# Leftover tokens of two batches interleaved token by token and stored in one transfer

## The chip, the core and the metric

The kernel runs on one core of one Trainium2 chip. The metric is the device time of one execution in microseconds (us), as the median of several runs. The engines are TensorE (PE in the profile; its weight loads are PEld), VectorE (DVE), ScalarE (ACT), GpSimd (POOL) and SyncE (SP). SyncE, ScalarE and GpSimd can issue DMA transfers; a transfer that an engine issues stands in that engine's own queue of instructions, shown as SPq, ACTq or POOLq.

## What is computed

An attention with landmark keys (8 batches, 8 heads, 576 tokens, 64 wide, 32 landmarks), and behind it a gated feed-forward block on all 4608 tokens. Cut to what matters:

```python
a = softmax(phi)                                  # over the 32 landmarks
k_m = einsum('bhsm,bhsd->bhmd', a, k)
v_m = einsum('bhsm,bhsd->bhmd', a, v)
attn = softmax(q @ k_m.T / sqrt(64))
x = (attn @ v_m), heads side by side              # 4608 x 512
g = x @ w_gate                                    # 512 x 1536
h = g * sigmoid(g) * (x @ w_val)
out = h @ w_out                                   # 1536 x 512, float32
```

Row `576 b + t` of the output is token t of batch b.

## The kernel before

The kernel goes through the eight batches one after the other. For each it forms the attention weights, multiplies them with a product of values and feed-forward weights (tiles `t_U`), and makes the hidden layer h, transposed, in three chunks of 512 hidden units: `hts[b, c]`, a tile `t_h` of 128 partitions x 4 x 576 tokens in bf16. A token's place in `t_h` is its half: `r = 0, 1` picks one of two blocks of 288, and token `2 t + r` of the batch stands at place `t` of block r.

The last product, h times `w_out`, is done with seven products of blocks in place of eight (a scheme of Strassen's kind). It works on 256 of the 288 tokens of each half. So 512 tokens of each batch go through `products(b, ...)`, and the last 64 tokens of each batch are left over. The leftovers of four batches together make one more such set of products, a "quad": `products(b, (), 0)` for batches 0 to 3, run beside batch 4, and `products(b, (), 1)` for batches 4 to 7, which runs at the very end of the kernel.

The steps that touch the leftovers, in the order in which they run:

- `chunk_done(b, c)` is called when a chunk of a batch's hidden layer is ready. Its inner function `ends` (L592) copies the 64 leftover columns of that chunk, on GpSimd, into the tile `t_x`, of which there is one for each pair of batches: `xs[b // 2]`, 128 partitions x 12 x 128 columns. There are 24 such copies (8 batches, 3 chunks), each of 128 x 256 elements. Which of the 128 columns belongs to which token is what the change is about.
- `quad_sums(qd)` forms sums and differences of the two `t_x` tiles of a quad on GpSimd, twelve instructions of 128 x 256 elements (L664 for the first three, L560 for the other nine), into the tiles `t_Q` and, in part, back into `t_x`.
- `products(b, by_hand, quad)` multiplies slices of `t_x` and `t_Q`, as weights of 128 columns, with halves of `w_out` or of its differences `t_T` (L727). A column of `t_x` is a partition of the result, so one result block of 128 partitions holds the leftover tokens of two batches, 64 each.
- `leftover(name, room, half, cols)` takes each of the four result blocks of a quad (two pairs of batches, two halves of 256 output columns) out of PSUM with VectorE (L796, L339) and stores it. Two transfers of 64 rows x 1 KB go out for one block, by `store_leftover` (L687). Both are issued on SyncE, but for three of the four blocks at the very end: there the second half is issued on ScalarE's queue.

The instructions stand on each engine's queue in the order in which the Python code calls them. Transfers from SyncE and ScalarE take eight completion semaphores in turn, and a transfer waits until the one eight places earlier has landed. The other stores are those of `store_block` (L683, 256 or 512 KB, SyncE); SyncE also issues transposing transfers for queries and keys (L117, L284). Loads go by GpSimd's queue. At the end of the program (L1113) SyncE waits for all outstanding transfers, one semaphore after the other.

Of the kernel before, what the change touches and what calls it, by code (L numbers as in the profile page):

```python
# [10 lines left out]
BF16 = mybir.dt.bfloat16  # L11
# [3 lines left out]
def kernel(  # L15
# [19 lines left out]
    nc = tc.nc  # L35
# [3 lines left out]
    B, H, S, D = q.shape  # L39
# [6 lines left out]
    NJF = DF // 128  # L46
# [11 lines left out]
    hpool = ctx.enter_context(tc.tile_pool(name="hpool", bufs=2))  # L58
# [5 lines left out]
    out_b = out.rearrange("(b t) c -> b t c", b=B)  # L64
# [16 lines left out]
    def done(*tiles):  # L81

        for t in tiles:
            free.append(held.pop(id(t))[0])
# [250 lines left out]
    def copy(eng, out, in_):  # L335
        if eng == "a":
            nc.scalar.copy(out=out, in_=in_)  # L337
        else:
            nc.vector.tensor_copy(out=out, in_=in_)  # L339
# [217 lines left out]
    xs, Ss, late = {}, {}, []  # L557

    def subtract(eng, out, x, y):
        eng.tensor_tensor(out=out, in0=x, in1=y, op=ALU.subtract)  # L560
# [20 lines left out]
    def blocks(b, c):  # L581

        x = hts[b, c].rearrange("p (m e) t -> p e m t", e=2)
        return [x[:, e, :, HALF * n:HALF * n + 256] for n in range(2) for e in range(2)]

    def chunk_done(b, c):

        if b % 2 == 0 and c == 0:
            xs[b // 2] = hpool.tile([128, NJF, 2, 64], BF16, tag="xs", name="t_x")

        def ends():
            nc.gpsimd.tensor_copy(  # L592
                out=xs[b // 2][:, 4 * c:4 * c + 4, b % 2].rearrange("p o (t r) -> p o t r", r=2),
                in_=hts[b, c].rearrange("p o (r t) -> p o t r", r=2)[:, :, 256:],
            )

        t = upool.tile([128, 4, 2, 256], BF16, tag=f"U{c}" if b == 1 else f"S{c}", name="t_S")
        Ss[b, c] = t
        A11, A12, A21, A22 = blocks(b, c)

        def sums(eng, part=(0, 1, 2, 3)):
            if 0 in part:
                eng.tensor_tensor(out=t[:, 0], in0=A21, in1=A22, op=ALU.add)  # L603
            terms = ((t[:, 0], A11), (A11, A21), (A12, t[:, 1]))
            for n in part:
                if n:
                    subtract(eng, t[:, n], *terms[n - 1])

        end = c + 1 == NCH
        fourth = b in (3, 7)  # L610
        if (b, c) in ((0, 2), (1, 1), (1, 2)):
            late.append(lambda *part: sums(nc.gpsimd if b else nc.vector, *part))
        elif b < 2:
            sums(nc.gpsimd)
        elif end:
            sums(nc.vector)
            if b + 1 == B:
                second.pop()(nc.vector, (2, 3))
                wait_for(Ss[b, 1][0:1, 3, 0, 0:1])
            else:  # L620
                wait_for(t[0:1, 3, 0, 0:1])
                second.pop()(nc.gpsimd, (3, 2))
        else:
            if c:
                sums(nc.gpsimd, (0, 1))
                second.append(sums)
            else:
                sums(nc.gpsimd)
        if end and b > 1 and not fourth:
            late.append(ends)  # L630
        else:
            ends()
        if b > 1 and c == 1:
            loads(b + 3)
        if b + 1 == B and end:
            quad_sums(1)
        if (b, c) in beside_sums:
            beside_sums[b, c]()
# [3 lines left out]
    def wait_for(x):  # L642

        t = att.tile([1, 1], BF16, tag="mark", bufs=1, name="t_mark")
        nc.gpsimd.tensor_copy(out=t, in_=x)

    def quad_sums(qd):

        x, y = xs[2 * qd], xs[2 * qd + 1]

        def quarters(c):
            return (
                z[:, 4 * c:4 * c + 4].rearrange("p (m e) a t -> p e m (a t)", e=2)[:, e]
                for z in (x, y) for e in range(2)
            )

        for c in range(NCH):
            Qs[qd, c] = att.tile([128, 3, 2, 128], BF16, tag=f"Q{c}", bufs=1, name="t_Q")
        for n in range(4):
            for c in range(NCH):  # L660
                t = Qs[qd, c]
                A11, A12, A21, A22 = quarters(c)
                if n == 0:
                    nc.gpsimd.tensor_tensor(out=t[:, 0], in0=A21, in1=A22, op=ALU.add)  # L664
                elif n == 1:
                    subtract(nc.gpsimd, t[:, 1], t[:, 0], A11)
                elif n == 2:
                    subtract(nc.gpsimd, A21, A11, A21)
                else:
                    subtract(nc.gpsimd, t[:, 2], A12, t[:, 1])  # L670
# [11 lines left out]
        for u in parts:  # L682
            nc.sync.dma_start(out=rows[:, u], in_=t_o[:, u, cols])  # L683

    def store_leftover(t_o, b, cols, eng):

        eng.dma_start(out=out_b[b, 512:S, cols], in_=t_o)  # L687

    def products(b, by_hand, quad=None):

        h = DM // 2
# [3 lines left out]
        end = quad == 1 or (quad is None and b + 1 == B)  # L695

        def A(e, n):
            if quad is not None:
                return lambda c, m, u: xs[2 * quad + n][:, 4 * c + 2 * m + e].rearrange(
                    "p a t -> p (a t)"  # L700
                )
            return lambda c, m, u: hts[b, c][
                :, 2 * m + e, HALF * n + 128 * u:HALF * n + 128 * u + 128
            ]

        def Sx(n):
            if quad is not None:
                return A(0, 1) if n == 2 else lambda c, m, u: Qs[quad, c][:, min(n, 2), m]
            return lambda c, m, u: Ss[b, c][:, n, m, 128 * u:128 * u + 128]
# [73 lines left out]
            both("o2", 256, slice(0, DM))  # L783

        def leftover(name, room, half, cols):
            engs = (nc.sync, nc.scalar if end and name != "c11" else nc.sync)

            def run():
                if room:
                    t = mine[room, "all"][:, half]  # L790
                else:
                    t = work.tile([128, h], FP32, tag="to", name="t_o")
                home = mine[dict(c11="a", c12="c").get(name, "s")]
                other = dict(c11="p1", c22="p5", c12="q6").get(name)
                if other:
                    nc.vector.tensor_tensor(  # L796
                        out=t, in0=home[:, 0], in1=mine[other][:, 0], op=ALU.add
                    )
                else:
                    copy("v" if end else "a", t, home[:, 0])  # L800
                if name != "c22":
                    done(home)
                for k in range(2):
                    x = 4 * quad + 2 * (name > "c20") + k
                    store_leftover(t[64 * k:64 * k + 64], x, cols, engs[k])

            return run

# [2 lines left out]
            c11=c11, c22=c22, c12=c12, c21=c21,  # L811
        )
        if quad is not None:
            ops.update(
                c11=leftover("c11", None, 0, lo), c12=leftover("c12", "q6", 1, hi),
                c22=leftover("c22", "p5", 1, hi), c21=leftover("c21", "q6", 0, lo),
            )
        now = {n: f for n, f in ops.items() if n not in by_hand}
        first = product("s", A(0, 0), W_(0, lo), "p1") + product("a", A(1, 0), W_(1, lo), "c11")
        five = product("c", Sx(0), T(0), "p5")  # L820
        six = product("s", Sx(1), T(1), "q6")
        three = product("c", Sx(3), W_(1, hi), "c12")
        seven = product("s", Sx(2), T(2), "c22")
        four = product("s", A(1, 1), T(3), "c21")
        if quad is not None or b + 1 == B:
            return first + six + five + seven + three + four, ops
# [155 lines left out]
    def loads(b):  # L982

        if b < B:
            load_q(b)
            load_phi(b, nc.gpsimd)
            load_k(b)
            load_v(b)
# [7 lines left out]
    for b in range(2, B):  # L996
# [60 lines left out]
        quad = []  # L1057
        if b == 4:
            quad = products(b, (), 0)[0]
# [58 lines left out]
```

## Time and profile before

| | us |
|---|---|
| median of 3 runs | 233.81 (233.22 to 233.97) |
| span of the profiled execution | 231.4 |
| TensorE matmul busy | 221.6 (96%) |
| VectorE busy | 185.1 (80%) |
| ScalarE busy | 171.7 (74%) |
| GpSimd busy | 140.8 (61%) |

The span runs from the first to the last instruction that the profile shows, and the measured time contains some more around it. The table below is from the list of DMA issues: how often each kind of store occurs, its size, and the median time from issue to landing.

| store | queue | times | KB each | us to landing |
|---|---|---|---|---|
| `t_o` (L683) | SyncE | 11 | 512 | 3.0 |
| `t_o` (L683) | SyncE | 10 | 256 | 4.5 |
| `t_q` (L687) | SyncE | 6 | 64 | 2.0 |
| `t_o` (L687) | SyncE | 4 | 64 | 2.6 |
| `t_p` (L687) | SyncE | 3 | 64 | 1.9 |
| `t_q` (L687) | ScalarE | 2 | 64 | 2.2 |
| `t_p` (L687) | ScalarE | 1 | 64 | 2.2 |

In the lines of the profile, `out<-in` names the tiles written and read, `L592` is line 592 of the kernel, and the names in `out_dram<-t_q` are those of the tile that is stored. A line of the windows view gives, for a stretch of time, the busy time and the number of instructions of each engine, the clock that TensorE was granted (1.00 is all of it), the busy share of the 16 DMA engines, and GB/s. A line of the waits view names who waited, for what, and the total, number and longest of these waits.

### The profile page before, as it was taken

How to read it: one execution, taken by the hardware profiler on the slowest of the kernel's cores; microseconds unless marked ns; L12 is line 12 of the kernel's file. 1: busy time of each engine (PE TensorE's matmuls, PEld its weight loads, DVE VectorE, ACT ScalarE, POOL GpSimd, SP SyncE). 2: the span in 40 equal slices, each digit the busy share in tenths (PEclk: the TensorE clock that was granted, in tenths of full speed). 3: DMA queues.
4: the chain of work that ended last, by engine and by line, in shares of the span. 5: the costliest groups of instructions: out<-in, count | busy, mean ns of one | idle time of the engine just before them, and what ended most of it. 6: DMA issues, size and time to landing. Idle time of an engine off the chain costs nothing.

```text
span 231.4 us, 7210 instructions
## 1 busy us (share of the span) xinstructions
PE 221.6 (96%) x2825; PEld 169.8 (73%) x2825; DVE 185.1 (80%) x423; ACT 171.7 (74%) x365; POOL 140.8 (61%) x190
## 2 busy tenths in 40 slices
PE   6987799999999999999999999999999999999993
PEld 2544476778887777878788787887788778878882
DVE  4245789999966799989997668998999899977732
ACT  2777898988447989968896658978898789677310
POOL 8422427998199049765977689464845394039291
PEclk9999999999999999999999999999999999999998
DMA  6999999999996992999299946994014502202125
GB/s 214 210 211 206 199 207 207 221 245 268 205 225 175 256 256 49 223 204 184 71 223 191 226 134 115 252 236 89 28 65 114 104 0 95 91 10 84 31 85 160
DMA packets 36674, 36.84 MB, mean 159 GB/s; under 512 B 14624, under 2 KB 31008, under 8 KB 36640
## 3 DMA queue, kind: packets, MB, share of 16 engines
q0 software_dynamic: 16272, 22.42, 52.5%
q1 hardware_dynamic: 19600, 13.18, 22.9%
q10 hardware_dynamic: 768, 0.79, 1.1%
q8 instruction: 22, 0.36, 0.6%
q14 instruction: 12, 0.10, 0.1%
HBM read 42.47 MB, written 9.44 MB: 224 GB/s over the span
## 4 chain that ended last, share of the span: by engine, by line
PE 86%; DMA 9%; POOL 2%; ACT 1%; issue 0%; DVE 0%; POOLq 0%
PE p_g L515 21%; PE p_os L727 21%; PE p_v L515 20%; PE p_oc L727 10%; DMA W<-in_moe_w_val_dram 9%; PE p_oa L727 5%; PE p_u L472 5%; PE p_kv L230 2%; PE p_g L396 1%; POOL t_kv L99 1%; POOL t_kv L103 1%; PE p_q L383 0%; POOL t_q L108 0%; ACT t_qT L337 0%; POOL W L138 0%
## 5 line engine op out<-in xcount | busy, mean ns | idle before, releaser
L538 DVE TENSOR_TENSOR t_h<-t_sg,p_v 128x288 bf16<-128x288 bf16 x192 | 81.8, 451 | 14.1 <-PE p_v L515 7.0
L515 PEld LDWEIGHTS <-t_U 128*128 128x128 bf16 x768 | 73.9, 98 | 21.2 <-issue 3.5
L532 ACT ACTIVATE t_sg<-p_g 128x288 bf16<-128x288 f32 x192 | 73.3, 424 | 17.1 <-PE p_g L515 11.4
L515 PE MATMUL p_g<-t_A,t_U 128*128 128x288 bf16 x384 | 77.0, 286 | 0.0
L515 PE MATMUL p_v<-t_A,t_U 128*128 128x288 bf16 x384 | 77.0, 286 | 0.0
L727 PEld LDWEIGHTS <-t_S 128*128 128x128 bf16 x384 | 37.5, 98 | 4.5 <-issue 0.2
L603 POOL TENSOR_TENSOR t_S<-t_h 128x512 bf16<-128x512 bf16 x17 | 19.7, 1157 | 32.7 <-DVE t_h L538 31.2
L727 PEld LDWEIGHTS <-t_h 128*128 128x128 bf16 x288 | 27.1, 98 | 8.6 <-issue 5.0
L492 ACT CAST t_U<-p_u 128x512 bf16<-128x512 f32 x51 | 27.0, 605 | 6.6 <-PE p_u L472 6.6
L727 PE MATMUL p_os<-t_T,t_S 128*128 128x256 bf16 x192 | 23.7, 273 | 0.0
L560 POOL TENSOR_TENSOR t_S<-t_S,t_h 128x512 bf16<-128x512 bf16 x17 | 19.6, 1156 | 1.3
L560 POOL TENSOR_TENSOR t_S<-t_h 128x512 bf16<-128x512 bf16 x16 | 18.4, 1152 | 0.0
L560 POOL TENSOR_TENSOR t_S<-t_h,t_S 128x512 bf16<-128x512 bf16 x16 | 18.4, 1152 | 0.0
L472 PE MATMUL p_u<-W,t_kT 64*32 64x512 bf16 (+1 forms) x416 | 15.3, 363 | 1.2 <-DMA W<-in_moe_w_gate_dram 0.6
L496 DVE CAST t_U<-p_u 128x512 bf16<-128x512 f32 x21 | 13.6, 683 | 1.9 <-PE p_u L472 1.9
L727 PE MATMUL p_os<-t_T,t_h 128*128 128x256 bf16 x96 | 14.8, 273 | 0.0
L875 PE MATMUL p_warm<-bones 128*128 128x512 bf16 x44 | 12.5, 421 | 1.7 <-DVE bones L897 1.7
L452 DVE TENSOR_TENSOR t_A<-t_E,t_lz 128x576 bf16<-128x576 bf16 x16 | 11.4, 740 | 0.7 <-ACT t_lz L428 0.7
L727 PE MATMUL p_oc<-t_T,t_S 128*128 128x256 bf16 x96 | 11.9, 273 | 0.0
L727 PE MATMUL p_oa<-WO,t_h 128*128 128x256 bf16 x96 | 11.8, 273 | 0.0
L727 PE MATMUL p_oc<-WO,t_S 128*128 128x256 bf16 x96 | 11.8, 272 | 0.1
L727 PE MATMUL p_os<-WO,t_h 128*128 128x256 bf16 x96 | 11.8, 273 | 0.0
(107 smaller groups left out, 308.3 us busy)
## 6 DMA issues: line engine op xcount, KB each, us to landing
out_dram<-t_o SPq DMA_DIRECT2D x11, 512.0 KB, 3.0
t_kv<-in_k_dram POOLq DMA_DIRECT2D x8, 576.0 KB, 10.5
t_q<-in_q_dram POOLq DMA_DIRECT2D x8, 576.0 KB, 8.4
t_kv<-in_v_dram POOLq DMA_DIRECT2D x8, 576.0 KB, 14.7
t_phi<-in_phi_dram POOLq DMA_DIRECT2D x6, 576.0 KB, 8.1
out_dram<-t_o SPq DMA_DIRECT2D x10, 256.0 KB, 4.5
WO<-in_moe_w_out_dram POOLq DMA_DIRECT2D x3, 512.0 KB, 19.2
W<-in_moe_w_gate_dram POOLq DMA_DIRECT2D x2, 512.0 KB, 16.5
```

The source lines that it names most:

```text
L230: nc.tensor.matmul(p[g][32 * i:32 * i + 32, 0:n], lhsT=phi_of(b, g, j, i), rhs=kvs[b][64 * g:64 * g + 64, w0:w1, i, j * D:(j + 1) * D], st ...
L452: nc.vector.tensor_tensor(out=a, in0=es.pop((b, g)), in1=lzs.pop((b, g)), op=ALU.mult)
L472: nc.tensor.matmul(p[g][32 * i:32 * i + 32, o:o + n], lhsT=kTs[b][64 * g:64 * g + 64, 2, 32 * i:32 * i + 32], rhs=w_part(w, c, i, g, halve ...
L492: nc.scalar.copy(out=t, in_=p)
L496: nc.vector.tensor_copy(out=t, in_=p)
L515: nc.tensor.matmul(p[:, 0:HALF], lhsT=Us[b, c, g][:, o // 2, which, 128 * (o % 2):128 * (o % 2 + 1)], rhs=atts[b, g][:, r], start=(g == 0) ...
L532: nc.scalar.activation(out=sg, in_=gate[:, 0:HALF], func=AF.Silu)
L538: nc.vector.tensor_tensor(out=dst, in0=sg, in1=val[:, 0:HALF], op=ALU.mult)
L560: eng.tensor_tensor(out=out, in0=x, in1=y, op=ALU.subtract)
L603: eng.tensor_tensor(out=t[:, 0], in0=A21, in1=A22, op=ALU.add)
L727: nc.tensor.matmul(mine[home][:, u], lhsT=lhs(c, m, u), rhs=rhs(c, m), start=fresh and u == 0, stop=(k == 5), skip_group_check=u == 1 or n ...
L875: nc.tensor.matmul(p[:, 0:128 * a], lhsT=bones, rhs=x.to_broadcast([128, a, 128]) if a > 1 else bones, start=True, stop=True,)
```

## The change

The two batches of a pair change their places in `t_x`. Before, the first 64 columns were the tokens of the even batch and the next 64 those of the odd one. Now column `2 t + a` is leftover token t of batch a of the pair. The copy in `ends` writes every second column, from column 0 or 1, where it wrote 64 columns side by side; what it reads is the same. `quad_sums` and `products` see the same 128 columns in the new order. A result block so has the tokens of both batches on alternate partitions, and one transfer takes the whole block: its SBUF side is 128 partitions of 1 KB, its side in memory is 64 tokens x 2 batches x 1 KB. All eight are issued on SyncE; `store_leftover` and the use of ScalarE's queue fall away. In the built programs SyncE has 39 transfers where it had 44, ScalarE one where it had four; the order of all other work on each engine is the same.

```diff
     def chunk_done(b, c):
         if b % 2 == 0 and c == 0:
-            xs[b // 2] = hpool.tile([128, NJF, 2, 64], BF16, tag="xs", name="t_x")
+            xs[b // 2] = hpool.tile([128, NJF, 64, 2], BF16, tag="xs", name="t_x")
         def ends():
             nc.gpsimd.tensor_copy(
-                out=xs[b // 2][:, 4 * c:4 * c + 4, b % 2].rearrange("p o (t r) -> p o t r", r=2),
+                out=xs[b // 2][:, 4 * c:4 * c + 4, :, b % 2].rearrange("p o (t r) -> p o t r", r=2),
                 in_=hts[b, c].rearrange("p o (r t) -> p o t r", r=2)[:, :, 256:],
             )
...
         def quarters(c):
             return (
-                z[:, 4 * c:4 * c + 4].rearrange("p (m e) a t -> p e m (a t)", e=2)[:, e]
+                z[:, 4 * c:4 * c + 4].rearrange("p (m e) t a -> p e m (t a)", e=2)[:, e]
...
-    def store_leftover(t_o, b, cols, eng):
-
-        eng.dma_start(out=out_b[b, 512:S, cols], in_=t_o)
-
...
                 return lambda c, m, u: xs[2 * quad + n][:, 4 * c + 2 * m + e].rearrange(
-                    "p a t -> p (a t)"
+                    "p t a -> p (t a)"
                 )
...
         def leftover(name, room, half, cols):
-            engs = (nc.sync, nc.scalar if end and name != "c11" else nc.sync)
-
...
-                for k in range(2):
-                    x = 4 * quad + 2 * (name > "c20") + k
-                    store_leftover(t[64 * k:64 * k + 64], x, cols, engs[k])
+                x = 4 * quad + 2 * (name > "c20")
+                nc.sync.dma_start(
+                    out=out_b[x:x + 2, 512:S, cols].rearrange("a t c -> t a c"), in_=t
+                )
```

## The prediction

> **What bounds the kernel now.** I read the busy table first, then TensorE over its working stretch, then the chain that ended last, then the end of the span queue by queue, because the change touches stores and one small copy only.
>
> ```profile
> PE 221.6 (96%) x2825; PEld 169.8 (73%) x2825; DVE 185.1 (80%) x423; ACT 171.7 (74%) x365; POOL 140.8 (61%) x190
> ```
>
> ```profile
> core 0: us, PE busy (x) PEld busy (x) DVE busy (x) ACT busy (x) POOL busy (x), PEclk, DMA share, GB/s
> 27.00:227.60 200.60, 200.50 (x2517) 158.58 (x2493) 172.00 (x381) 153.77 (x336) 129.23 (x169) 1.00 0.74 154
> ```
>
> From 27.0 to 227.6 us TensorE is busy for 200.50 of 200.60 us at a granted clock of 1.00. No store and no GpSimd copy holds it up there. What the change saves in that stretch on any other queue is therefore worth nothing, unless it takes something away from TensorE. The order of TensorE's instructions is the same in both programs. The end, from 227.6 us on, is where a store can be seen:
>
> ```profile
> 226.88 0.73 PE p_os L727 x6
> 227.64 0.42 DVE t_q L339
> ```
>
> ```profile
> 223.68 0.38 SPq L683 DMA_DIRECT2D out_dram<-t_o  x1
> 226.76 0.47 SPq L687 DMA_DIRECT2D out_dram<-t_p  x1
> 226.76 0.55 ACTq L687 DMA_DIRECT2D out_dram<-t_p  x1
> 227.37 0.50 SPq L687 DMA_DIRECT2D out_dram<-t_q  x1
> 227.41 0.75 ACTq L687 DMA_DIRECT2D out_dram<-t_q  x1
> 228.14 0.47 SPq L687 DMA_DIRECT2D out_dram<-t_q  x1
> 228.28 0.54 ACTq L687 DMA_DIRECT2D out_dram<-t_q  x1
> ```
>
> The chain ends with the last product (227.6), VectorE's copy out of PSUM (ends 228.06) and two stores of 64 KB, one on SyncE's queue and one on ScalarE's. Columns are start, duration, engine, line. From issue to landing they take:
>
> ```profile
> out_dram<-t_o SPq DMA_DIRECT2D x1, 256.0 KB, 2.1
> out_dram<-t_q SPq DMA_DIRECT2D x1, 64.0 KB, 2.0
> out_dram<-t_q ACTq DMA_DIRECT2D x1, 64.0 KB, 2.2
> ```
>
> The landing events behind these rows are, to two places: SyncE 228.14 + 1.95 = 230.09, ScalarE 228.28 + 2.16 = 230.44. So ScalarE's half sets the end; it starts 0.14 later and takes 0.21 longer. SyncE waits for all stores one after the other:
>
> ```profile
> SPq L1113 <- DMA out_dram<-t_q: 1.0, 2, 0.7
> ```
>
> The span is 231.44 us, so 1.00 us follows the last landing. In the events ScalarE's semaphore is the last but one that SyncE asks for, and one more step of 0.06 us stands behind it. The median of the three runs, 233.81, lies 2.37 us above the span; I carry that over unchanged.
>
> **The change, part by part.** *Sixteen transfers become eight.* Eight leftover blocks went out as sixteen transfers of 64 KB: thirteen on SyncE, three on ScalarE. Now there are eight of 128 KB, all on SyncE. For the first quad, four pairs between 131.6 and 141.8 us become four singles: SyncE's queue gets some 4 x 0.59 = 2.4 us shorter. Behind them stand a 512 KB store and a transpose that feeds batch 5. They may start 0.6 us earlier, which TensorE's full stretch hides. The pair at 215.15 (1.12 us) has SyncE idle behind it until 218.81. Worth 0.
>
> *The end.* ScalarE loses three issues, 0.55 + 0.75 + 0.54 = 1.84 us; nothing is queued behind them but the end of the program. The last store is now one SyncE issue at 228.14, as before (it waits for VectorE, not for the queue, while one issue takes less than 0.7 us). Its form, 128 partitions on one side and 64 steps of 2 rows on the other, is in no row, so I bound issue to landing from both sides. How fast the halves move is seen here:
>
> ```profile
> 224.50:225.50 1.00, 1.00 (x11) 0.88 (x10) 0.47 (x1) 0.37 (x1) 1.00 (x2) 1.00 0.77 262
> 227.80:228.70 0.90, 0.00 (x0) 0.00 (x0) 0.26 (x1) 0.00 (x0) 0.00 (x0) 1.00 0.76 180
> ```
>
> The last two numbers are the share of the DMA engines and GB/s. The 256 KB store from 128 partitions (first line) moves 262/0.77 = 340 GB/s when busy, which over 16 engines is 48 ns for a row of 1 KB. The stores from 64 partitions (second) move 180/0.76 = 237 GB/s, 69 ns a row. One block has 128 rows, 8 for each engine; a half has 4; the 256 KB store has 16. Low bound: the 256 KB row less eight rows, 2.13 - 8 x 0.048 = 1.75. High bound: SyncE's half plus its whole stretch of movement again (0.45 us in the packet records), 1.95 + 0.45 = 2.40. The nearest row is the 256 KB one (same partitions, same 1 KB rows). But the outer count of 64 belongs to the slower issues: 0.47 against 0.38, and the first row moved 1.12 against 0.89 us after the start. I add that 0.23 to the low bound: 1.98. So landing at 228.14 + 1.98 = 230.12, against 230.44: -0.32. The 0.06 step behind ScalarE's semaphore falls away, since the last semaphore is now the last asked for: -0.38 in all. With the bounds, -0.61 to +0.04.
>
> The Trainium skill, DMA: Bandwidth & Descriptors, has two places that bear on this. "Rules for kernel authors" says not to split a transfer into partition halves, on two queues either, because both share the same engines; the rows of 69 and 48 ns go with it, and it speaks for the change. Its fit in "Anatomy of one DMA", about 2.0 us plus bytes over 436 GB/s (for GpSimd's path), speaks against: 131072 bytes make an estimate of 2.30 us, a landing at 230.44, and a gain of nothing but the 0.06. The measured 256 KB store took 2.13 where the fit says 2.60, so I go by the trace.
>
> *The copy on GpSimd.* All 24 copies of leftover columns now write every second element:
>
> ```profile
> L592 POOL COPY t_x<-t_h 128x256 bf16<-128x256 bf16 x24 | 10.3, 435 | 0.0
> L664 POOL TENSOR_TENSOR t_Q<-t_x 128x256 bf16<-128x256 bf16 x6 | 3.8, 658 | 0.0
> ```
>
> The number of elements stays 256, and the source was read with a stride already, so I take 0 more. No row shows a strided write; bounds are 0 and the 0.22 to the two-input row of the same size (a packed write gone could even double 0.41; that is a rival). The cover: until 210 us GpSimd's work is hidden under TensorE. In the last batch only the copy at 218.36 counts, since GpSimd waits 4.2 us for VectorE before it. Twelve sums follow back to back, and the last is close to its reader:
>
> ```profile
> 224.38 1.92 POOL L560 TENSOR_TENSOR t_Q<-t_x,t_Q 128x256 bf16<-128x256 bf16 x3
> 226.06 0.82 PE L727 MATMUL p_oc<-WO,t_Q 128*128 128x256 bf16 x6
> ```
>
> It ends at 226.30. The fifth of these six products begins at 226.50 and its weights load 0.1 earlier, so 0.1 us is spare. A copy 0.22 longer would push the end by 0.12.
>
> *Sum.* -0.38 + 0 + 0: span 231.06, time 231.06 + 2.37 = 233.43. With the bounds, -0.61 + 0 and +0.04 + 0.12: 233.2 to 234.0.
>
> **The rivals.** *The new form is slow to issue (slower).* The place is SyncE's queue after 226.76. Three leftover stores follow each other there, and if an issue takes X, the third starts at 226.8 + 2X + waits. What speaks for it: both sides of every SyncE copy so far have the same counts, here they differ (128 against 64 x 2), and the 64-count issue is already the dearer one. Against: no plain issue on SyncE after 80 us exceeds 0.6 us but one of 1.03, behind traffic. If an issue costs as much as the pair it replaces, 1.12 to 1.19, the three start at 226.76, 227.99 and 229.22; the last ends at 230.41 and lands some 1.5 to 1.8 later (1.95 - 0.47, and up to 0.28 for four more rows), near 232.05. That is +1.6 us, 235.4. It decides (over 0.70 us) from X of about 0.9 on. The same price would come from a transfer spread over few engines.
>
> *GpSimd's strided write costs double.* 0.41 more on the copy at 218.36, less the 0.1 spare, holds the last products up by 0.31 and eats the gain: 233.43 + 0.31 = 233.7. For it: it is an untried form on an engine with 0.1 us of slack. Against: it moves one element per partition at a time anyway by its 0.41 us for 256, as far as a duration can tell.
>
> *The transfer is as long as ScalarE's half.* Twice as many rows in one queue at 69 ns land at 2.30 to 2.40: the end stays, 233.8.
>
> *More gain than I see.* Over 0.70 us faster would need a landing at 229.7, 1.6 us after the issue, faster than any store in the trace. Only scatter (the three runs span 0.75 us) or another chip's run can give that.
>
> **How the numbers follow.** Forecast 0.47, copy dear 0.12, no gain 0.10, slow issue 0.22, more gain 0.09. A change under 0.3% (0.70 us) can't be told from none in such measurements. Forecast, copy and no gain lie all within it, but for scatter: same 0.62. Faster 0.14 is the last case and 0.05 of scatter from the forecast. Slower 0.24 is the slow issue and 0.02 of scatter. The predicted time is 233.5, the forecast's 233.43 rounded. The range reaches from 232.9 (forecast's low end and 0.3 of scatter) to 235.3, nearly the whole of the slow issue.
>
> **What would show it.** Right: eight SyncE stores of 128 KB, each issued in 0.4 to 0.6 us and landing within 1.75 to 2.4; none on ScalarE; 27 to 227.6 us still full; the copies at 0.41; the last landing 230.0 to 230.4. Wrong: issues over 0.9 us, a gap before the last eighteen products, or any new wait of TensorE in the middle.

## The result, and the profile after

| | median us | runs | range of the runs |
|---|---|---|---|
| before | 233.41 | 21 | 233.07 to 234.00 |
| changed | 232.94 | 21 | 232.75 to 233.66 |

The ratio is 0.9985 with an interval of [0.9978, 0.9991]: the change gains 0.15%, about 0.35 us (0.2 to 0.5 by the interval; the medians differ by 0.47). That is a gain, but within the 0.3% named in the prediction as no change. The profiled execution of the changed kernel has a span of 231.18 us, where the kernel before had 231.44.

The page's busy table of the changed kernel is nearly the old one:

```profile
PE 222.2 (96%) x2825; PEld 170.0 (74%) x2825; DVE 184.8 (80%) x423; ACT 171.4 (74%) x365; POOL 141.4 (61%) x190
```

Two windows of the changed kernel follow, TensorE's working stretch and half a microsecond in which only the last store moves:

```profile
27.00:227.60 200.60, 200.50 (x2517) 158.59 (x2501) 171.72 (x381) 153.62 (x336) 129.86 (x169) 1.00 0.72 154
229.40:229.90 0.50, 0.00 (x0) 0.00 (x0) 0.00 (x0) 0.00 (x0) 0.00 (x0) 1.00 0.78 260
```

TensorE is as full as before, 200.50 of 200.60 us, so nothing was gained or lost in the middle. In the second line 260 GB/s at a share of 0.78 is 333 GB/s when busy. Over 16 engines that makes 49 ns for a row of 1 KB. The new store moves at the rate of the 256 KB stores, not at the 69 ns of the old halves.

The end of the changed kernel in the timeline (start, duration, engine, line; then idle time ahead and its releaser):

```profile
224.48 1.91 POOL L560 TENSOR_TENSOR t_Q<-t_x,t_Q 128x256 bf16<-128x256 bf16 x3
...
226.14 0.81 PE L723 MATMUL p_oc<-WO,t_Q 128*128 128x256 bf16 x6
...
226.84 0.55 SPq L798 DMA_DIRECT2D out_dram<-t_p  x1
...
227.48 1.27 SPq L798 DMA_DIRECT2D out_dram<-t_q  x2
227.72 0.42 DVE L339 COPY t_q<-p_os 128x256 f32<-128x256 f32 x1 [0.30 <-PE p_os L723]
```

GpSimd's last sum ends at 226.39, inside the six products that read it, and holds none of them up. One transfer goes out for each block, on SyncE alone; the line "x2" holds the issues at 227.48 and 228.20, of 0.56 and 0.54 us. The list of DMA issues (KB each, median us to landing) and the wait at the end, both of the changed kernel:

```profile
out_dram<-t_q SPq DMA_DIRECT2D x4, 128.0 KB, 2.1
out_dram<-t_p SPq DMA_DIRECT2D x2, 128.0 KB, 2.1
```

```profile
SPq L1108 <- DMA out_dram<-t_q: 0.5, 1, 0.5
```

A store of 128 KB lands about as soon after its issue as the 256 KB one did before (2.1). SyncE now waits for one landing where it waited for two.

To compare kernels at a few tenths of a microsecond I use three events of each trace: the end of VectorE's last copy out of PSUM, the landing of the last store (its last semaphore event), and the end of the span. What comes before the copy is TensorE's chain, whose end differs by 0.12 us between the two profiles of the changed kernel (the copy ends at 228.14 and, in c1 below, at 228.26); what follows it is the tail that the change works on. Microseconds:

| kernel | copy ends | copy to last landing | landing to end | copy to end |
|---|---|---|---|---|
| before | 228.06 | 2.38 | 1.00 | 3.38 |
| changed | 228.14 | 2.12 | 0.92 | 3.04 |

The tail is 0.34 shorter: 0.26 by the store, 0.08 behind its landing. That is as much as the measured gain of 0.35.

The packet records of the two profiles divide the 0.26. Counted from the end of the copy, ScalarE's half was issued after 0.22 us and the new store after 0.06. The first row moves 1.27 and 1.19 us after the issue, the rows take 0.45 and 0.52, and the landing follows the last row by 0.44 and 0.35. So the rows of the new store take 0.07 longer than those of the half. What is gained is that the half on ScalarE, which was issued later and took longer to its first row and from its last row to the landing, is no longer needed, and what makes that possible is that 128 rows take little longer than 64; at the pace of the halves they would take about 0.9 (an estimate, 2 x 0.45).

### The profile page after: what moved, and what is told of

It reads as the page before. It is cut to its first block, busy times and chain, and to the rows that moved or that the text cites. A ratio compares the mean times of both kernels' runs of the same rounds, so it can differ in the third digit from the quotient of the medians.

```text
span 231.2 us, 7197 instructions
## 1 busy us (share of the span) xinstructions
PE 222.2 (96%) x2825; PEld 170.0 (74%) x2825; DVE 184.8 (80%) x423; ACT 171.4 (74%) x365; POOL 141.4 (61%) x190
## 4 chain that ended last, share of the span: by engine, by line
PE 86%; DMA 9%; POOL 2%; ACT 1%; issue 0%; DVE 0%; POOLq 0%
PE p_g L515 21%; PE p_os L723 21%; PE p_v L515 20%; PE p_oc L723 10%; DMA W<-in_moe_w_val_dram 9%; PE p_oa L723 5%; PE p_u L472 5%; PE p_kv L230 2%; PE p_g L396 1%; POOL t_kv L99 1%; POOL t_kv L103 1%; PE p_q L383 0%; POOL t_q L108 0%; ACT t_qT L337 0%; POOL W L138 0%
## 5 line engine op out<-in xcount | busy, mean ns | idle before, releaser
L870 PE MATMUL p_warm<-bones 128*128 128x512 bf16 x44 | 13.3, 444 | 1.7 <-DVE bones L892 1.7
L723 PE MATMUL p_os<-t_T,t_h 128*128 128x256 bf16 x96 | 14.8, 273 | 0.0
```

The source lines that it names most:

```text
L723: nc.tensor.matmul(mine[home][:, u], lhsT=lhs(c, m, u), rhs=rhs(c, m), start=fresh and u == 0, stop=(k == 5), skip_group_check=u == 1 or n ...
L870: nc.tensor.matmul(p[:, 0:128 * a], lhsT=bones, rhs=x.to_broadcast([128, a, 128]) if a > 1 else bones, start=True, stop=True,)
```

## The experiments

All twelve in one table, with the same three intervals and with the time against the kernel before, measured beside it. (For b4 the copy is VectorE's half of it.)

| run | copy to landing | landing to end | copy to end | median us | ratio to before |
|---|---|---|---|---|---|
| a1_end_only | 2.16 | 1.16 | 3.33 | 233.34 | 0.9993 [0.9982, 1.0004] |
| a2_first_only | 2.27 | 1.70 | 3.97 | 233.99 | 1.0025 [1.0014, 1.0035] |
| a3_halves | 2.44 | 0.97 | 3.42 | 233.52 | 0.9997 [0.9986, 1.0007] |
| a4_two_steps | 9.13 | 0.94 | 10.07 | 248.81 | 1.0665 [1.0640, 1.0690] |
| c1_changed_again | 2.13 | 0.92 | 3.05 | 232.91 | 0.9981 [0.9972, 0.9989] |
| x1_one_more | 2.12 | 1.84 | 3.95 | 233.94 | 1.0021 [1.0010, 1.0032] |
| x2_first_only_four_more | 2.34 | 0.97 | 3.31 | 233.55 | 0.9999 [0.9986, 1.0012] |
| x3_end_only_four_more | 2.52 | 0.93 | 3.45 | 233.49 | 1.0008 [0.9993, 1.0024] |
| x4_end_only_four_fewer | 2.12 | 0.94 | 3.06 | 233.18 | 0.9993 [0.9972, 1.0014] |
| b1_sync_halves | 4.19 | 0.92 | 5.10 | 235.42 | 1.0086 [1.0065, 1.0107] |
| b2_copy_twice | 2.13 | 0.94 | 3.07 | 233.45 | 0.9997 [0.9982, 1.0013] |
| b4_copy_shared | 2.44 | 0.92 | 3.37 | 233.29 | 0.9991 [0.9977, 1.0005] |

**The last quad alone, the first quad alone.** If the gain is the last store's, changing only batches 4 to 7 keeps it and changing only batches 0 to 3 loses it.

```diff
-            xs[b // 2] = hpool.tile([128, NJF, 64, 2], BF16, tag="xs", name="t_x")
+            xs[b // 2] = hpool.tile([128, NJF, 128], BF16, tag="xs", name="t_x")
...
+    TOGETHER = (1,)        # a1_end_only;  (0,) in a2_first_only
+    def by_batch(b):
+        form = "p j (t a) -> p j a t" if b // 4 in TOGETHER else "p j (a t) -> p j a t"
+        return xs[b // 2].rearrange(form, a=2)
...
+                if quad in TOGETHER:
                     nc.sync.dma_start(
                         out=out_b[x:x + 2, 512:S, cols].rearrange("a t c -> t a c"), in_=t
                     )
+                    return
+                engs = (nc.sync, nc.scalar if end and name != "c11" else nc.sync)
+                for k in range(2):
+                    engs[k].dma_start(out=out_b[x + k, 512:S, cols], in_=t[64 * k:64 * k + 64])
```

> New order of columns and single stores for batches 4 to 7 alone; batches 0 to 3 as before. Theory (the gain is made after the last product, by the last store): all of it, 0.3 to 0.4 us under the kernel before (ratio 0.9985), last landing about 2.1 us after the end of VectorE's last copy against 2.38 before. Rival (the gain comes from SyncE's shorter queue between 131 and 142 us): 0.0, ratio 1.000.

> New order and single stores for batches 0 to 3 alone; the end of the kernel as before, with three halves on ScalarE's queue. Theory: no gain, ratio 1.000 within 0.001; SyncE's queue 2 us shorter between 131 and 142 us, TensorE full there as before. Rival (SyncE's queue in the middle): 0.9985.

The store did what was expected in both. In a1 it lands 2.16 after the copy (2.12 in the changed kernel), in a2 the old pair takes 2.27 (2.38 before). The whole did not follow: the tail of a1 is 3.33, hardly shorter than the 3.38 of before (its time, 0.9993, lies in an interval that holds the whole gain and none), and a2 is slower than before. The table says where it went: behind the landing, 1.16 and 1.70 us in place of 0.92. So I listed what SyncE does there. It asks for the semaphores of the last transfers one after the other, in a fixed order (the walk, below). These are the times at which the trace has each request, which is when its semaphore has come (the number is the semaphore's):

```
before  106 228.65  108 229.13  109 229.22  113 229.29  114 229.35  115 229.64  116 229.70  117 230.46  118 230.52
changed 106 228.79  108 228.85  109 228.91  113 228.98  114 229.07  115 229.14  116 229.64  117 229.73  118 230.28
a1      106 228.91  108 228.98  109 229.47  113 229.69  114 230.42  115 230.48  116 230.55  117 230.61  118 230.67
a2      106 229.59  108 230.58  109 230.65  113 231.29  114 231.36  115 231.85  116 231.93  117 232.00  118 232.06
```

Two things are in this list. Each request costs 0.06 to 0.09 us, so it matters on which semaphore the last landing falls. In the changed kernel it is 118, the last asked for (landing 230.26, request 230.28). In a1 it is 114 (230.40), with four requests behind it; in a2 it is 113 (231.28), with five. And in each list one step of 0.49 to 0.50 us has no landing to wait for: 106 to 108 before, 115 to 116 in the changed kernel, 108 to 109 in a1, 114 to 115 in a2. Counted along SyncE's recorded instructions it always follows the 79th. Before and after the change it lies while SyncE would wait for the last landing anyway; in a2 it lies behind the landing and is paid. Both places depend on the number of transfers in the whole program. The semaphores are given out in turn, in rounds of eight. The kernel before has 48 transfers on SyncE and ScalarE, six rounds; the changed kernel has 40, five rounds, so its last store is on 118 again. a1 and a2 have 44, and end half way through a round. Neither kernel changed only what it was meant to.

**The walk tested.** Four kernels change that number by splitting or joining 512 KB stores in the middle, where TensorE is full. x1 is the changed kernel with one transfer more, 41 in all, so that the last store falls on 108, the first of the eight asked for. x2 and x3 are a2 and a1 with four more (48), x4 is a1 with four fewer (40).

```diff
-        parts = [slice(u, u + 1) for u in range(2)] if b < 2 else [slice(0, 2)]
+        apart = b < 2 or (b, n) in ((6, 1),)                              # x1
+        apart = b < 2 or (b, n) in ((4, 1), (5, 1), (6, 0), (6, 1))       # x2, x3
+        parts = [slice(u, u + 1) for u in range(2)] if apart else [slice(0, 2)]
...
+        parts = [slice(0, 2)]                                             # x4
```

> The changed kernel, but the 512 KB store of batch 6 near 207 us goes out as two of 256 KB. Nothing stands behind it on SyncE for 8 us. It makes one transfer more, so the last store falls on the first of the eight completion semaphores that SyncE asks for at the end, not on the last. Theory (where the last store stands in that order counts, 0.06 us for each semaphore asked for after it, and a pause of about 0.45 us in SyncE's queue there may come out from under the landing): 0.43 to 0.9 us slower than the changed kernel, ratio to before 1.0004 to 1.0024. Rival (only the transfer counts): as the changed kernel, 0.9985.

> The changed kernel once more, beside the three that follow. Ratio 0.9985 within 0.0008 by every theory.

Measured in the same set of runs: 233.94 against 232.91, so one transfer more costs 1.03 us (0.93 by the two ratios), nearly three times what the change gains. The wait view of x1, to be held against the 0.5 of the changed kernel:

```profile
SPq L1109 <- DMA out_dram<-t_q: 1.4, 1, 1.4
```

SyncE waits longer because it now waits at the first of the eight. In the events the landing is at 230.10, then the requests for 108 to 118 stand at 230.12, .19, .25, .32, .81, .89, .96 and 231.02: seven steps, and the pause of 0.46 again between 114 and 115, behind the 79th instruction. Together they take 0.91 us.

> New form for batches 0 to 3 alone, as in the run that came out at 1.0025, but four 512 KB stores after 160 us go out as two of 256 KB each, so that the last stores fall on the same semaphores as in the kernel before. Theory (that run lost its 0.58 us in the walk through the semaphores at the end): 1.000 within 0.001. Rival (the new form itself holds TensorE up near 135 us): still 1.002 to 1.003.

x2's tail is 3.31 and its ratio is back at 0.9999. The loss of a2 was the walk and the pause, not the old stores and not the new form in batches 0 to 3.

> New form for batches 4 to 7 alone, with the same four stores split, so that the last store falls on the last semaphore asked for, as in the changed kernel, where it was the fourth of eight. Theory: the whole gain, 0.9985 within 0.001, against 0.9993 without the four. Rival (half of the gain comes from batches 0 to 3): 0.9993 again.

This one missed: 1.0008 where 0.9985 was expected. The walk is short (0.93 behind the landing), as planned, but the landing itself is late, 2.52 behind the copy. The timeline of x3:

```profile
228.11 1.64 SPq L805 DMA_DIRECT2D out_dram<-t_q  x2
228.32 0.42 DVE L339 COPY t_q<-p_os 128x256 f32<-128x256 f32 x1 [0.30 <-PE p_os L729]
```

The pair of issues that takes 1.27 us in the changed kernel takes 1.64 here. The first is over at 228.65, the copy ends at 228.75, and the last store is issued at 229.20 only. With four transfers more, the 79th instruction is the last store but one, and the pause stands right ahead of the last store. I had moved the semaphore and overlooked that the pause moves too.

> New form for batches 4 to 7 alone, and the stores of batches 0 and 1 whole (512 KB) where they went out as two, so four transfers fewer than in the end-only run: the last store again falls on the last semaphore asked for, and the pause of about 0.45 us in SyncE's queue, which has stood ahead of its 82nd instruction in all traces so far, falls between the last two of these semaphores, under the landing. (With four transfers more, the 82nd instruction was the last store itself.) Theory (the whole gain is made by the last store, if the pause stays hidden): 0.9983 within 0.001, 3.05 us from the end of VectorE's last copy to the end of the span. Rival (batches 0 to 3 bring part of the gain): 0.9993 or more.

By time x4 decides nothing: its interval holds 0.9985 and 1 alike. Its profile has the tail that was expected, 3.06, with the last store on 118 and nothing paid behind it. (The place that the expectation counts as the 82nd is the 80th of the instructions that the trace records, the one behind the 79th as above.) So changing the last quad alone gives the whole shorter tail if the count comes out well; that its time does too is not shown.

**Interleaved, but still in two halves.** a3 keeps the new layout and splits each block into two transfers of 64 partitions (32 tokens x 2 batches), the second on ScalarE's queue as before.

```diff
-                nc.sync.dma_start(
-                    out=out_b[x:x + 2, 512:S, cols].rearrange("a t c -> t a c"), in_=t
-                )
+                engs = (nc.sync, nc.scalar if end and name != "c11" else nc.sync)
+                for k in range(2):
+                    rows = slice(512 + 32 * k, 544 + 32 * k)
+                    engs[k].dma_start(
+                        out=out_b[x:x + 2, rows, cols].rearrange("a t c -> t a c"),
+                        in_=t[64 * k:64 * k + 64])
```

> New order of columns everywhere, but each block still goes out in two transfers of 64 partitions, 32 tokens of both batches each, the second halves at the end on ScalarE's queue. Theory: no gain, ratio 1.000 within 0.001 (last landing 2.3 to 2.4 us after VectorE's last copy), and 69 ns for a row of 1 KB; the interleaving itself is worth nothing. Rival (the new order of columns or of rows in memory is what is faster): 0.9985 or part of it.

The time is that of before, 0.9997 [0.9986, 1.0007], and the tail 3.42. The window of its last stores:

```profile
228.10:229.00 0.90, 0.00 (x0) 0.00 (x0) 0.17 (x1) 0.00 (x0) 0.00 (x0) 1.00 0.77 184
```

184 GB/s at a share of 0.77 is 239 GB/s when busy, 69 ns a row: the rate of the old halves. That two halves move side by side is not the reason: in b1 below, where they follow each other on SyncE alone, the rows of one half still take 0.45 to 0.47 us in the packet records, against 0.51 to 0.53 for the twice as many rows of the new store. A window of b1 in which only its last half moves:

```profile
231.80:232.20 0.40, 0.00 (x0) 0.00 (x0) 0.00 (x0) 0.00 (x0) 0.00 (x0) 1.00 0.67 154
```

That is 230 GB/s when busy, 71 ns a row. So the order of the tokens in itself gives nothing; it is the single transfer over all 128 partitions that moves its rows faster and makes ScalarE's half unnecessary.

**One transfer, but not interleaved.** a4 keeps the layout of before and stores a block as 2 batches x 64 tokens in one transfer.

```diff
-                for k in range(2):
-                    x = 4 * quad + 2 * (name > "c20") + k
-                    store_leftover(t[64 * k:64 * k + 64], x, cols, engs[k])
+                x = 4 * quad + 2 * (name > "c20")
+                nc.sync.dma_start(out=out_b[x:x + 2, 512:S, cols], in_=t)
```

> Order of columns as before, each block in one SyncE transfer whose side in memory is 2 batches x 64 tokens. Theory (what makes the single transfer good is its spread over all DMA engines; the outer count of 64 allows that, an outer count of 2 allows two engines): the last store takes 64 rows of 48 to 70 ns on each engine, 3.1 to 4.5 us, and lands 4.5 to 6 us after its issue; the three last stores queue up behind each other, 3 to 10 us slower than before. Rival (any single transfer of 128 partitions moves at 48 ns a row over all engines): as fast as the changed kernel, ratio 0.9985.

It is 15.2 us slower, more than the 3 to 10 that I expected. A window of a4's end:

```profile
239.00:245.00 6.00, 0.00 (x0) 0.00 (x0) 0.00 (x0) 0.00 (x0) 0.00 (x0) 0.62 0.14 48
```

A store of the same 128 KB, which moved at 260 GB/s in the changed kernel, moves at 48, at a share of 0.14, close to 2 of 16 engines (0.125). The last three stores land 4.98, 7.10 and 9.06 us after their issues, one behind the other. That makes the tail 6.7 us longer. The rest is in the middle, where the timeline of TensorE in a4 has

```profile
150.75 0.71 PE L727 MATMUL p_oc<-WO,t_S 128*128 128x256 bf16 x5
157.05 1.22 PE L727 MATMUL p_os<-t_T,t_S 128*128 128x256 bf16 x5 [5.59 <-ACT t_q L752]
```

TensorE waits 5.59 us for ScalarE, whose copy waits until a slow store of the first quad has left the `t_q` buffer. The windows of a4 behind this wait show the granted clock:

```profile
150.00:157.00 7.00, 1.46 (x14) 1.17 (x12) 2.39 (x5) 1.12 (x2) 3.59 (x7) 0.86 0.99 175
...
158.00:159.00 1.00, 1.00 (x7) 0.67 (x6) 0.00 (x0) 0.30 (x1) 0.00 (x0) 0.50 0.45 139
...
162.00:164.00 2.00, 2.00 (x21) 1.42 (x20) 1.69 (x4) 1.52 (x5) 0.00 (x0) 1.00 0.79 127
```

For some five microseconds TensorE runs at half its clock. The tail (6.7), the wait (5.6) and about 2.5 for the clock (an estimate, half of five) make 14.8 of the 15.2. I had counted the slow transfer at the end and not the buffer that it holds in the middle. The Trainium skill, DMA: Bandwidth & Descriptors, section "Why a DMA increments its semaphore by 16 and not by 1", says that a transfer spreads over the largest number of engines, up to 16, that divides the slowest dimension of both its sides. That gives 2 for a4's memory side of 2 x 64 and 16 for the interleaved one of 64 x 2; the share of 0.14 agrees.

**Without ScalarE's queue, without the interleaving.** b1 is the kernel before with both halves on SyncE.

```diff
-            engs = (nc.sync, nc.scalar if end and name != "c11" else nc.sync)
+            engs = (nc.sync, nc.sync)
```

> The kernel before, with both halves of each block on SyncE at the end too. Theory: SyncE issues six halves of 0.47 to 0.58 us one after the other from 226.8 us, the last at about 229.6, and the pause falls on the last store: landing 231.6 to 232.1, 1.2 to 1.6 us slower than before, ratio 1.005 to 1.007. Rival (ScalarE's queue is what made the end late, and leaving it out is the gain): 0.9985 to 1.000.

By the ratio it is 2.0 us slower (1.0086 [1.0065, 1.0107]), by the medians 1.8, by the tail 1.7. The timeline of b1's last six issues:

```profile
227.10 1.11 SPq L687 DMA_DIRECT2D out_dram<-t_p  x2
...
228.32 2.80 SPq L687 DMA_DIRECT2D out_dram<-t_q  x4
```

Six issues of 0.47 to 0.60 us follow each other on SyncE, and the last block, whose copy ended at 228.40, waits for its turn: its stores are issued at 230.02 and 230.55. The pause of 0.46 us, which the expectation put ahead of the last store, falls between the fourth and the fifth issue (229.56 to 230.02). Without it the sixth issue begins 2.99 us after the first, where the expectation had 2.8; with that the loss goes beyond the expected 1.2 to 1.6.

**The strided copy on GpSimd.** In the changed kernel's groups by line, the copies of leftover columns, one for each batch and chunk, read

```profile
L592 POOL COPY t_x<-t_h 128x256 bf16<-128x256 bf16 x24 | 11.5, 489 | 0.0
```

against 435 ns before; the shortest is 408 before and 462 now, so writing every second element costs 0.05 to 0.06 us. To see what a longer copy would do, b2 makes the last one twice, ahead of the last sums.

```diff
             ends()
+            if b + 1 == B and end:
+                ends()
```

> The changed kernel, with GpSimd's copy of the last chunk of the last batch done twice, 0.41 us more ahead of the twelve sums. Theory (0.1 us is spare before TensorE waits): the last products and the end 0.3 us later, ratio to before 0.9996 to 1.0000. Rival (the copy is hidden, whatever it costs): 0.9983.

The time is 0.9997 [0.9982, 1.0013], an interval that holds both theories; the traces decide. The last copy in the changed kernel and the two in b2:

```profile
218.44 0.47 POOL L592 COPY t_x<-t_h 128x256 bf16<-128x256 bf16 x1
218.92 1.00 POOL L592 COPY t_x<-t_h 128x256 bf16<-128x256 bf16 x2
```

TensorE in b2:

```profile
226.63 0.60 PE L725 MATMUL p_oc<-WO,t_Q 128*128 128x256 bf16 x4
...
227.47 0.39 PE L725 MATMUL p_oc<-WO,t_Q 128*128 128x256 bf16 x2 [0.23 <-POOL t_Q L560]
```

The group of six products of the changed kernel is broken: the last two wait for GpSimd's last sum. The 0.23 is only the idle time behind the product before them, which overlaps its neighbours; from the start of the six products to the end of the last product of the kernel, b2 takes 1.89 us and the changed kernel 1.54. So 0.53 more on GpSimd costs 0.35, close to the 0.3 that was expected; some 0.18 us were spare, and the 0.06 of the strided write hides in that.

**A try at something better.** b4 shares the last PSUM copy between VectorE and ScalarE, 128 columns each.

```diff
-                    copy("v" if end else "a", t, home[:, 0])
+                    if end:
+                        w = t.shape[-1] // 2
+                        copy("v", t[:, 0:w], home[:, 0, 0:w])
+                        copy("a", t[:, w:], home[:, 0, w:])
```

> The changed kernel, with the very last copy out of PSUM (128 x 256, 0.42 us on VectorE) shared: VectorE copies 128 columns, ScalarE the other 128. Theory (from the last product on everything is in one chain): the last store is issued 0.1 to 0.2 us earlier and the kernel ends as much earlier, ratio to before 0.9976 to 0.998. Rival (something else holds the end): 0.9983.

```profile
227.99 0.29 DVE L339 COPY t_q<-p_os 128x128 f32<-128x128 f32 x1 [0.30 <-PE p_os L723]
228.37 0.27 ACT L337 COPY t_q<-p_os 128x128 f32<-128x128 f32 x1 [2.00 <-DVE t_q L339]
```

The timeline of b4 shows the two halves one after the other: ScalarE's half was released by VectorE's, not by the product. The store is issued at 228.66; behind a whole copy by VectorE it would have been 227.99 + 0.42 + 0.06 = 228.47. So the expected gain did not come. No version that I ran is shown to beat the changed kernel.

## Why the prediction was right, point by point

The forecast, no change that can be told, with a small gain from the last store, is what happened; 232.94 lies in the range.

*The sum against the profiled execution.* Its term of -0.38 measured -0.34. The last store: -0.32 predicted, -0.26 measured, because the landing came 2.06 after the issue and not 1.98 (0.02 came back, as the issue followed the copy 0.06 later and not 0.08). The 0.08 lies ahead of the first row: the issue itself took 0.54, where I had reckoned with the 0.47 of the old 64-row store, and the first row moved 1.19 after it began, not 1.12. The rows took 0.52, as the sum had it (0.90 of the 256 KB store less 0.38). The step behind ScalarE's semaphore: -0.06 predicted, -0.08 measured.

*The median above the span.* This term was mis-sized. I carried over 2.37 us, from a median of three runs (233.81) and a span from another run. The kernel before has a median of 233.41 in 21 runs, and runs with both numbers have less between them: the changed kernel 232.96 and 231.18, a1 233.37 and 231.57, x1 233.71 and 231.93, 1.8 us each. The span of 231.44 and 1.8 make 233.2, the lowest of the three runs; the median of the three stood 0.6 above that. With 1.8 the predicted span of 231.06 gives 232.9. The forecast of 233.43 is 0.49 above the 232.94 measured: 0.57 too much here, less 0.12 by which the span was longer than predicted, and 0.04 of scatter.

*Worth 0 in the middle.* Right on average: the working stretch has the same 200.50. "0 more" for the strided copy was wrong in size (+0.06 each) and right in effect, and the spare time ahead of the last products is nearer to 0.2 than to the 0.1 that I read.

*The -0.06 step was read without its reason.* I took from the trace of before that one request stood behind ScalarE's semaphore and none behind SyncE's, and carried SyncE's place over without asking what sets it. It stayed because the change takes away eight transfers, one whole round of semaphores, and the pause stayed under the landing. That was luck: nothing in the prediction looked at either. One transfer more would have put the last store at the other end of the walk, and x1 shows the price: 1.03 us, which would have made the change slower than before. This rival the prediction lacked, and the trace of before had both its parts: the steps of 0.06 us, and 0.49 us between 106 and 108 with no landing due.

*The rivals.* The slow issue: 0.54 to 0.56 us at the end, far from the 0.9 where it would have decided. a4 shows what its other half, "spread over few engines", costs when it does happen: far more than the 1.6 that I gave it. Copies at double cost: 0.06, not 0.41. A transfer as long as ScalarE's half: the rival had the landing 2.30 to 2.40 after the issue, by 69 ns a row, the forecast 1.98; measured are 2.06 and 49 ns a row, which is the forecast's reason.

## What to carry to other kernels

At the end of this kernel, one transfer over all 128 partitions beat two over 64 on two queues, with 64 steps as the slowest dimension of its side in memory; with 2 steps there it was by far the slowest. Interleaving the batches is what gave the 64. Before crediting a change of a few tenths of a microsecond, list what the engine that closes the program does behind the last landing: a transfer more or less anywhere on these two queues shifts which semaphore is last and what stands ahead of the last store, and here that was worth up to 1.03 us. A test that changes the number of transfers needs a control that restores it.

## What the runs showed of the hardware that was not expected

*The pause.* Behind the 79th instruction that the trace records of SyncE, 0.45 to 0.47 us pass with nothing running there. It is to be seen in twelve of the fourteen profiles, in front of a request or of a store; in a4 and x4 a wait for a landing covers the place. That it goes with the position in SyncE's program and not with a wait is shown by x1, x3 and b1. What it is stays open. Loading of instructions would fit a fixed position. No packet of the two queues called "instruction" lies inside the pause, but in all fourteen profiles an 8 KB packet of one of them (q14) starts 1.08 to 1.32 us after that 79th instruction ends, in a4 and x4 too, although the instruction ends at 237.60 in a4 and between 228.65 and 231.39 elsewhere. So the packet goes with the same place in the program as the pause; that the one causes the other is not shown.

*Stalls of TensorE at 135 us.* In five of the fourteen profiles TensorE stops once near 135 us, always ahead of the same product. In a2, on TensorE's timeline:

```profile
134.93 0.41 PE L515 MATMUL p_v<-t_A,t_U 128*128 128x288 bf16 x2
136.04 0.49 PE L728 MATMUL p_oc<-t_T,t_Q 128*128 128x256 bf16 x3 [0.69 <-issue]
```

"issue" says that no semaphore held it up. The page of the changed kernel has a DMA queue for this kind of traffic (packets, MB, share):

```profile
q8 instruction: 22, 0.36, 0.6%
```

Its 22 packets have 16 KB each, and one of them lies near 132 us in every run. Its start and TensorE's stall, in us:

```
b1  132.84  0.17        a2  133.48  0.70
a4  133.12  0.32        before, changed and seven others  131.96 to 132.72  none
b2  133.17  0.42
x3  133.33  0.39
```

Every start after 132.8 has a stall and no earlier one has, and the latest start has the longest. In all fourteen the packet comes behind a transposing transfer (L117) whose issue takes 7.0 to 8.2 us, longest in x3 and a2; that it makes the packet late, and that the late packet makes the stall, was not tested. The Trainium skill, Runtime: NRT & Kernel Launch, section "Instruction fetch mechanics", says that the sequencer fetches its program in blocks of 16 KB on a queue of its own and that this is mostly hidden; here it fits the packets, and if the stalls are theirs, "mostly" leaves 0.17 to 0.70 us that are not hidden in five of fourteen. These stalls may be part of the scatter of the runs (a2's fall into 233.8 to 234.1 and 234.5 to 234.8, and its profile with the stall is the 234.76).

*ScalarE's store.* Halves of equal size landed 1.95 after an issue on SyncE and 2.16 after one on ScalarE in the kernel before, and 2.0 and 2.2 in a3. In the packet records of before, the first row of the last half moves 1.12 us after the issue on SyncE and 1.27 after that on ScalarE, and the landing follows the last row by 0.37 and 0.44. ScalarE's half always had one of SyncE's beside it, so whether its queue or this neighbour costs the 0.2 is open.
